# A gated recurrence and a maxout MoE, rebuilt around 128 tokens of eight heads

## The chip, the core and the metric

The kernel runs on one core of a Trainium2 chip. The metric is the device time of one launch in microseconds. Five engines take instructions from queues of their own and meet through semaphores: PE multiplies matrices (its weight loads are a row of their own, PEld, in the profile), DVE is the vector engine, ACT the scalar engine, POOL the GpSimd, and SP issues transfers. Matrix products land in PSUM, everything else lies in SBUF; both have 128 partitions.

## The reference

The first half is a gated linear recurrence for 4 batches and 8 heads over 768 tokens with 48 columns a head. Its output, eight heads side by side, is the 3072 x 384 input of a maxout layer.

```python
for t in range(S):                                 # attention; state is 48 x 48 a head
    state = alpha[:, :, t, :, None] * state + np.einsum('bhd,bhe->bhde', k[:, :, t], v[:, :, t])
    y[:, :, t] = np.einsum('bhd,bhde->bhe', q[:, :, t], state)

x = np.ascontiguousarray(attn_out.transpose(0, 2, 1, 3)).reshape(B * S, H * D)
h1 = x @ w1                                        # w1, w2: 384 x 1024
h2 = x @ w2
g = np.maximum(h1, h2)
return (g @ w_out).astype(np.float32)              # w_out: 1024 x 384
```

Inputs, weights and output are 32-bit floats.

## The kernel before

The recurrence is cut into chunks of 128 tokens. Inside a chunk it is a masked product of scaled queries and keys, between chunks a 48 x 48 state is carried. `gla_head` does all of this for one head of one batch: four loads of 768 x 48, six chunks in two groups of three, then one or two transfers that put the head's result into its partitions of `xT`, the transposed input of the MoE. It is called 32 times, and everything in it is 48 wide.

For a head: the logarithm of alpha (L86) and its sums to the chunk's end (L91, then the exponential `Rt` of L93) give the scaled keys `KL` (POOL, L102). For a group: three products with `mrec` give the logarithms' running sums in each chunk, already transposed (`csA`, L114), measured from the chunk's middle so that both signs of the exponential stay small; ACT takes both (`AAm`, L122 and L123) and the chunk's decay (`ALE`, L126). For a chunk: two transposes of q and k into 48 partitions (`qkT`, L131 and L132), a scaling (`QKs`, L134), the scores `pp` (L136), the mask (`PTm`, L138), the scaled queries for the state (`QA2`, L140), two products into `yt` (L141, L142), the state's increment (L143) and the new state (L145). The scheduler of the tile framework sets the order on each engine from the dependencies; buffers from pools (most with two or three turns) bound how far heads overlap.

When all heads are done, the PSUM pool is released and the MoE follows in six windows of 512 tokens: for each of eight slices of 128 columns three products with w1 and three with w2 (L194, L196), a copy of the first half by ACT (L198), the maximum on DVE (L199); then 32 products with w_out (L204), a copy (L209) and the store (L210). The weights are loaded first of all, on SP's queue, and cast by POOL (L65 to L67).

Logarithm and exponential are in different tables of ACT, and each change of function loads one (the ACT_TABLE_LOAD rows).

Of the kernel before, what the change touches and what calls it, by code (L numbers as in the profile page):

```python
# [8 lines left out]
FP16 = mybir.dt.float16  # L10
FP32 = mybir.dt.float32

@with_exitstack
def kernel(
# [10 lines left out]
):  # L26
    nc = tc.nc
# [3 lines left out]
    G = 3  # L31
    NG = NCH // G
    NT, DM = out.shape
    DFF = moe_w1.shape[1]

    constp = ctx.enter_context(tc.tile_pool(name="constp", bufs=1))
    wtp = ctx.enter_context(tc.tile_pool(name="wtp", bufs=1))
    xtp = ctx.enter_context(tc.tile_pool(name="xtp", bufs=1))

    ident16 = constp.tile([128, 128], FP16)  # L40
    make_identity(nc, ident16)
    u16 = constp.tile([128, 128], FP16)
    make_upper_triangular(nc, u16, val=1.0, diag=True)
    l16 = constp.tile([128, 128], FP16)
    make_lower_triangular(nc, l16, val=1.0, diag=False)
    CW = 132
    mrec = constp.tile([128, CW], FP16)
    ones64 = constp.tile([128, 128], FP16)
    nc.gpsimd.memset(ones64, 0.0)
    nc.gpsimd.memset(ones64[0:64, :], 1.0)  # L50
    nc.gpsimd.memset(mrec, 0.0)
    nc.vector.tensor_sub(out=mrec[:, 0:128], in0=u16, in1=ones64)
    nc.gpsimd.memset(mrec[:, 128:129], 1.0)
    nc.gpsimd.memset(mrec[0:64, 129:130], 1.0)

    w1f = wtp.tile([128, 3, DFF], FP32)
    w2f = wtp.tile([128, 3, DFF], FP32)
    wof = wtp.tile([128, 8, DM], FP32)
    nc.sync.dma_start(out=w1f, in_=moe_w1.rearrange("(s p) f -> p s f", p=128))
    nc.sync.dma_start(out=w2f, in_=moe_w2.rearrange("(s p) f -> p s f", p=128))  # L60
    nc.sync.dma_start(out=wof, in_=moe_w_out.rearrange("(s p) d -> p s d", p=128))
    w116 = wtp.tile([128, 3, DFF], FP16)
    w216 = wtp.tile([128, 3, DFF], FP16)
    wo16 = wtp.tile([128, 8, DM], FP16)
    nc.gpsimd.tensor_copy(out=w116, in_=w1f)  # L65
    nc.gpsimd.tensor_copy(out=w216, in_=w2f)
    nc.gpsimd.tensor_copy(out=wo16, in_=wof)  # L67

    xT = xtp.tile([128, 3, NT], FP16)

    glap = ctx.enter_context(tc.tile_pool(name="glap", bufs=3))
    glas = ctx.enter_context(tc.tile_pool(name="glas", bufs=4))
    glps = tc.alloc_tile_pool(name="glps", bufs=2, space=bass.MemoryType.PSUM)

    def gla_head(b, h):
        qf = glap.tile([128, NCH, D], FP32, tag="qf")
        kf = glap.tile([128, NCH, D], FP32, tag="kf")
        vf = glap.tile([128, NCH, D], FP32, tag="vf")
# [24 lines left out]

        S16 = glas.tile([D, D], FP16, tag="S16")
        nc.vector.memset(S16, 0.0)

        YTsb = glap.tile([D, NG, G * C], FP16, tag="YTsb")

        for g in range(NG):
            csA = glps.tile([D, G * CW], FP32, tag="csA")  # L110
            yt = glps.tile([D, G * C], FP32, tag="yt")
            for jj in range(G):
                c = g * G + jj
                nc.tensor.matmul(  # L114
                    csA[:, jj * CW : (jj + 1) * CW],
                    lhsT=loga[:, c, :],
                    rhs=mrec,
                    start=True,
                    stop=True,
                )  # L120
# [7 lines left out]
            for jj in range(G):  # L128
# [112 lines left out]
```

## Time and profile before

| | |
|---|---|
| median of 3 runs | 414.44 us (414.21 to 414.57) |
| span of the profiled execution | 412.1 us |
| PE busy, matmuls | 343.6 us, 1856 |
| DVE busy, instructions | 250.9 us, 977 |
| ACT busy, instructions | 202.9 us, 390 |
| POOL busy, instructions | 45.9 us, 82 |
| bytes moved by DMA | 31.05 MB in 107,855 packets, 101,424 of them under 512 bytes |
| granted clock of PE | 1.000 |

The span runs from the first to the last instruction. Matmuls are pipelined and their ends modelled, so a matmul's record is longer than what it keeps PE from doing; what one costs in a row of its kind is the distance from start to start. The share of busy time is a mean over a recurrence stage and a MoE stage with different limits.

### The profile page before, as it was taken

The numbers are of one execution on the slowest core, as the hardware profiler recorded it, in microseconds if no ns is written. First come the engines' busy times: TensorE is split into PE (matmuls) and PEld (weight loads), VectorE is DVE, ScalarE is ACT, GpSimd is POOL, SyncE is SP. The second block draws the span as 40 slices with busy tenths as digits, with TensorE's granted clock in tenths as the row PEclk, the third lists the DMA queues.
The fourth block names the chain that finished last, engine by engine and source line by source line (L and its number), as shares of the span: only waits on it lengthen the run. The fifth ranks groups of instructions, "written<-read, shape, count | busy, mean of one in ns | idle before, by whom it ended". The sixth has DMA issues, their size and how long they took to land. (4 is left out here: it accounts for less than half of the span.)

```text
span 412.1 us, 5933 instructions
## 1 busy us (share of the span) xinstructions
PE 343.6 (83%) x1856; PEld 181.5 (44%) x1856; DVE 250.9 (61%) x977; ACT 202.9 (49%) x390; POOL 45.9 (11%) x82
## 2 busy tenths in 40 slices
PE   0036888888888888888888888888898999999996
PEld 0013444444444444444444444444443545545543
DVE  0134777777777777777777777777884342442441
ACT  0148656556556556656556656656201344344342
POOL 4330111112111111111111111111100000000000
PEclk9999999999999999999999999999999999999999
DMA  7992253333443333443333444211000012012012
GB/s 291 280 173 43 59 105 69 67 64 67 90 97 75 64 66 65 85 99 77 66 64 64 86 96 81 51 36 37 10 13 9 21 58 76 19 59 76 21 59 76
DMA packets 107855, 31.05 MB, mean 75 GB/s; under 512 B 101424, under 2 KB 107056, under 8 KB 107824
## 3 DMA queue, kind: packets, MB, share of 16 engines
q1 hardware_dynamic: 54192, 16.52, 18.1%
q10 hardware_dynamic: 53632, 14.16, 15.5%
q8 instruction: 14, 0.23, 0.2%
q14 instruction: 17, 0.14, 0.1%
HBM read 23.59 MB, written 4.72 MB: 69 GB/s over the span
## 5 line engine op out<-in xcount | busy, mean ns | idle before, releaser
L131 PE MATMUL qkT<-ident,q 128*48 128x128 f16 x192 | 57.7, 301 | 23.7 <-DVE q L99 23.7
L138 DVE TENSOR_TENSOR PTm<-pp,u 128x128 f16<-128x128 f32 x192 | 54.8, 286 | 31.2 <-PE pp L136 22.6
L199 DVE TENSOR_TENSOR gT<-h1s,h2p 128x512 f16<-128x512 f16 x48 | 33.0, 688 | 58.1 <-ACT h1s L198 30.2
L122 ACT ACT_TABLE_LOAD x30 | 38.5, 1283 | 48.8 <-DVE QKs L134 47.6
L122 ACT ACTIVATE AAm<-csA 48x396 f16<-48x396 f32 x64 | 31.6, 494 | 59.5 <-DVE QKs L134 58.8
L132 PE MATMUL qkT<-ident,k 128*48 128x128 f16 x192 | 60.3, 314 | 0.0
L143 PE MATMUL aux<-vh,KL 128*48 128x48 f16 x192 | 45.6, 238 | 16.0 <-POOL KL L102 12.4
L141 PE MATMUL yt<-PTm,vh 128*48 128x128 f16 x192 | 52.4, 273 | 7.1 <-DVE PTm L138 5.6
L134 DVE TENSOR_TENSOR QKs<-qkT,AAm 48x256 f16<-48x256 f16 x192 | 52.9, 276 | 6.4 <-ACT AAm L123 1.9
L136 PE MATMUL pp<-QKs 48*128 48x128 f16 x192 | 54.7, 285 | 0.0
L86 ACT ACT_TABLE_LOAD x31 | 39.8, 1283 | 19.1 <-POOL vh L101 18.6
L198 ACT CAST h1s<-h1p 128x512 f16<-128x512 f32 x48 | 28.1, 586 | 42.1 <-PE h1p L194 42.1
L114 PE MATMUL csA<-mrec,loga 128*48 128x132 f16 x192 | 34.2, 305 | 17.2 <-ACT ALE L126 13.8
L142 PE MATMUL yt<-QA,S16n 48*48 48x128 f16 x160 | 47.8, 299 | 0.0
L143 PEld LDWEIGHTS <-KL 128*48 128x48 f16 x192 | 28.2, 147 | 42.4 <-POOL KL L102 24.1
L140 DVE TENSOR_SCALAR QA<-QKs,ALE 48x128 f16<-48x128 f16 x192 | 46.2, 241 | 0.0
L145 DVE SCALAR_TENSOR_TENSOR S16n<-S16n,ALE,aux 48x48 f16<-48x48 f16 x160 | 39.7, 248 | 7.3 <-PE aux L143 7.1
L131 PEld LDWEIGHTS <-q 128*48 128x48 f16 x192 | 21.7, 113 | 45.9 <-DVE q L99 23.7
L194 PE MATMUL h1p<-xT,w 128*128 128x512 f16 x144 | 40.2, 389 | 0.6 <-DVE YTsb L154 0.6
L154 DVE CAST YTsb<-yt 48x384 f16<-48x384 f32 x64 | 35.2, 550 | 8.4 <-PE yt L142 1.6
L196 PE MATMUL h2p<-xT,w 128*128 128x512 f16 x144 | 39.7, 385 | 0.0
L101 POOL CAST vh<-vf 128x288 f16<-128x288 f32 x32 | 13.6, 424 | 234.3 <-issue 228.0
(43 smaller groups left out, 370.4 us busy)
## 6 DMA issues: line engine op xcount, KB each, us to landing
kf<-in_k_dram ACTq DMA_DIRECT2D x32, 144.0 KB, 3.3
vf<-in_v_dram ACTq DMA_DIRECT2D x32, 144.0 KB, 3.3
qf<-in_q_dram SPq DMA_DIRECT2D x32, 144.0 KB, 2.6
af<-in_alpha_dram SPq DMA_DIRECT2D x32, 144.0 KB, 3.1
out_dram<-outs ACTq DMA_DIRECT2D x24, 192.0 KB, 1.9
xT<-YTsb SPq DMA_DIRECT2D x24, 72.0 KB, 3.1
w1f<-in_moe_w_dram SPq DMA_DIRECT2D x1, 1536.0 KB, 6.8
w2f<-in_moe_w_dram SPq DMA_DIRECT2D x1, 1536.0 KB, 10.7
```

The costliest lines, as they stand in the source:

```text
L86: nc.scalar.activation(out=loga, in_=af, func=mybir.ActivationFunctionType.Ln)
L122: nc.scalar.activation(out=AAm[:, 0, :], in_=csA, func=mybir.ActivationFunctionType.Exp, scale=1.0)
L131: nc.tensor.transpose(qkT[:, 0, :], q16[:, c, :], ident16)
L132: nc.tensor.transpose(qkT[:, 1, :], k16[:, c, :], ident16)
L134: nc.vector.tensor_mul(out=QKs, in0=qkT, in1=AAm[:, :, jj * CW : jj * CW + C])
L136: nc.tensor.matmul(pp, lhsT=QKs[:, 1, :], rhs=QKs[:, 0, :], start=True, stop=True)
L138: nc.vector.tensor_mul(out=PTm, in0=pp, in1=u16)
L140: nc.vector.tensor_scalar(out=QA2, in0=QKs[:, 0, :], scalar1=ALE[:, jj, 1:2], scalar2=None, op0=mybir.AluOpType.mult)
L141: nc.tensor.matmul(yt[:, jj * C : (jj + 1) * C], lhsT=vh[:, c, :], rhs=PTm, start=True, stop=False)
L142: nc.tensor.matmul(yt[:, jj * C : (jj + 1) * C], lhsT=S16, rhs=QA2, start=False, stop=True)
L143: nc.tensor.matmul(pst, lhsT=KL[:, c, :], rhs=vh[:, c, :], start=True, stop=True)
L194: nc.tensor.matmul(h1p, lhsT=w116[:, ds, fsl], rhs=xT[:, ds, tkn], start=(ds == 0), stop=(ds == 2))
```

## The change

A unit of work is now 128 tokens of one batch with all eight heads: 24 units (`gla(i)`), each with four loads that bring tokens into partitions and heads into columns. Operands are padded: each head of the logarithm, q and k has 64 columns, 48 in use, in tiles that are zeroed once, so that two heads fill 128 columns and are transposed by one instruction.

The running sum `cs` is one product for eight heads, not transposed; q and k are scaled before the transpose (`qn` on DVE, `kn` on POOL). Four products with two columns (`dps`) give the decay of each half of the chunk. After eight transposes DVE copies all of `tp` at once to `qk`. Each pair of heads then has the first head in partitions 0 to 47 and the second in 64 to 111, and the eight score products alternate between them. The state is carried for pairs: increment `kv`, `tm` on DVE, the next chunk's scaled state `sb` on POOL.

The result is built transposed, directly as MoE input. Values (`vp`) and states (`sb`) stand in wide zeroed tiles, and `vwin` and `swin` take windows of 128 columns from them in which a head's 48 columns fall where they belong in `x`. Products of several heads so accumulate into the same `yp`, sixteen a unit, ten where no state comes in. The transfers to `xT` are gone; ACT copies `yp` to `xt`.

The maxout uses max(a, b) = b + relu(a - b): the kernel forms w12 = w1 - w2 (L143) and w2o = w2 w_out (L137) once, so that a window takes one product with w12, a relu (ACT and DVE in turn), the product with w_out, and x w2o on top. A window is 256 tokens, and `moe(w)` is called after unit 2w + 3, between the units. ACT names one table at the start that holds logarithm and exponential.

All loads are on SP's queue: units 0 and 1, the weights (w2, w_out, w1), then the other units, with buffers for eight.

```diff
-    for b in range(B):
-        for h in range(H):
-            gla_head(b, h)
-    glps.release()
+    nc.scalar.preload_act_table_set("natural_log_exp_and_others")
+    def load(i):
+        b, c = divmod(i, NCH)
+        t = {}
+        for name, src in (("af", alpha), ("kf", k), ("qf", q), ("vf", v)):
+            t[name] = ldp.tile([128, H, D], FP32, tag=name, name=name)
+            nc.sync.dma_start(out=t[name], in_=src[b, :, c * C : (c + 1) * C, :].rearrange("h p d -> p h d"))
+        loads[i] = t
...
+    def vwin(t, h, ds):
+        p = 128 + h * VS - (D * h - 128 * ds)
+        return t[:, p : p + 128]
...
+    def gla(i):
...
+        nc.scalar.activation(out=lg[:, :, 0:D], in_=t["af"], func=ACTF.Ln)
+        nc.gpsimd.tensor_copy(out=vd, in_=t["vf"])
...
+        nc.tensor.matmul(csv, lhsT=mrec, rhs=lg[:, :, 0:D], start=True, stop=True)
+        for j in range(HP):
+            nc.tensor.matmul(
+                dps[:, j, :], lhsT=lg[:, 2 * j : 2 * j + 2, :].rearrange("p h w -> p (h w)"), rhs=halves,
+                start=True, stop=True,
+            )
...
+        nc.scalar.activation(out=Em, in_=csv, func=ACTF.Exp, scale=-1.0)
+        nc.scalar.activation(out=Ep, in_=csv, func=ACTF.Exp)
...
+        nc.scalar.activation(out=de, in_=dps, func=ACTF.Exp)
+        nc.gpsimd.tensor_mul(out=kn[:, :, 0:D], in0=t["kf"], in1=Em)
+        nc.vector.tensor_mul(out=qn[:, :, 0:D], in0=t["qf"], in1=Ep)
+        tp = psp.tile([128, 2, HP, C], FP16, tag="g", bufs=3, name="tp")
...
+        qk = gp.tile([128, 2, HP, C], FP16, tag="qk", name="qk")
+        nc.vector.tensor_copy(out=qk, in_=tp)
...
+                nc.gpsimd.tensor_mul(
+                    out=sd[r, :, e], in0=tm[r], in1=dd[r, :].unsqueeze(2).to_broadcast([64, HP, D])
+                )
...
+        for j in range(HP):
+            for a in range(2):
+                r = slice(64 * a, 64 * a + D)
+                nc.tensor.matmul(pa[a][:, j, :], lhsT=qk[r, 1, j, :], rhs=qk[r, 0, j, :], start=True, stop=True)
+        for a in range(2):
+            nc.vector.tensor_mul(
+                out=pt[:, a], in0=pa[a], in1=u16.unsqueeze(1).to_broadcast([128, HP, C])
+            )
...
+            mms += [(vwin(vp, h, ds), pt[:, h % 2, h // 2, :]) for h in range(H) if ds in touches(D * h, D)]
...
+    def moe(w):
...
+                    nc.tensor.matmul(
+                        hp[:, n, :], lhsT=w12[:, ds, f * 128 : (f + 1) * 128],
+                        rhs=xt[:, ds].rearrange("p n t -> p (n t)"), start=(ds == 0), stop=(ds == ND - 1),
+                    )
+            if f2 % 2 == 0:
+                nc.scalar.activation(out=gT[:, 2 * f2 : 2 * f2 + 2, :], in_=hp, func=ACTF.Relu)
+            else:
+                nc.vector.tensor_relu(out=gT[:, 2 * f2 : 2 * f2 + 2, :], in_=hp)
...
+                nc.tensor.matmul(op, lhsT=xt[:, ds, n, :], rhs=w2o[:, ds, :], start=(ds == 0), stop=False)
...
+    for i in range(NI):
+        if i + 2 < NI:
+            load(i + 2)
+        gla(i)
+        if i == 1:
+            weights()
+        if i % 2 == 1 and i // 2 - LAG >= 0:
+            moe(i // 2 - LAG)
```

The scheduler puts the instructions of two units and one MoE window into one another. On PE before, in mid-recurrence, one step of a head reads:

```order
L131 LDWEIGHTS q_987
L131 MATMUL qkT<-ident_64,q_987 48x128
L132 LDWEIGHTS k_988
L132 MATMUL qkT<-ident_64,k_988 48x128
L143 LDWEIGHTS KL
L143 MATMUL aux<-vh,KL 48x48
L141 LDWEIGHTS vh
L141 MATMUL yt<-PTm,vh 48x128
L142 LDWEIGHTS S16n
L142 MATMUL yt<-QA_1092,S16n 48x128
L136 LDWEIGHTS QKs
L136 MATMUL pp<-QKs 128x128
```

Afterwards, in unit 4 (counted from 0) with MoE window 1, PE has these rows between the last transpose of q (L177 stands ahead of two more hp) and the scores `pp` (L219), where `op` is the MoE's output:

```order
L258 LDWEIGHTS xt
L258 MATMUL op<-w2o,xt 128x384
L258 LDWEIGHTS xt
L258 MATMUL op<-w2o,xt 128x384
L258 LDWEIGHTS xt
L258 MATMUL op<-w2o,xt 128x384
L260 LDWEIGHTS gT
L260 MATMUL op<-wo_147,gT 128x384
L260 LDWEIGHTS gT
L260 MATMUL op<-wo_147,gT 128x384
L219 LDWEIGHTS qk
L219 MATMUL pp<-qk 128x128
```

The scores of a unit now stand behind five products of the MoE, which wait for nothing of that unit. In the same place the four transposes of kn stand behind ten hp products, and those of qn behind twelve more and the four kv.

On ACT before, at a change of head, with a table load at each change of function:

```order
L86 ACT_TABLE_LOAD
L86 ACTIVATE loga<-af 128x288
L82 DMA vf<-in_v_dram 128x6x48
L81 DMA kf<-in_k_dram 128x6x48
L122 ACT_TABLE_LOAD
L122 ACTIVATE AAm<-csA 48x396
L123 ACTIVATE AAm<-csA 48x396
L126 ACTIVATE ALE<-csA 48x6
L122 ACTIVATE AAm<-csA 48x396
L123 ACTIVATE AAm<-csA 48x396
```

Afterwards, from unit 3's exponentials to unit 4's:

```order
L167 ACTIVATE Em<-cs 128x384
L168 ACTIVATE Ep<-cs 128x384
L170 ACTIVATE de<-cs 128x8
L236 CAST xt<-yp 128x3x128
L153 ACTIVATE lg_123<-af 128x8x48
L263 COPY outs<-op 128x384
L236 CAST xt<-yp 128x3x128
L263 COPY outs<-op 128x384
L167 ACTIVATE Em<-cs 128x384
L264 DMA out_dram<-outs 128x2x384
L168 ACTIVATE Ep<-cs 128x384
L170 ACTIVATE de<-cs 128x8
```

Em and Ep of unit 3 come ahead of the copy of unit 2's result (the first `xt`), but those of unit 4 stand behind the copy of unit 3's, and the store of a MoE window stands between Em and Ep.

## Rows read from the trace of the kernel before

**Rows 1.** The page, part 1: busy time, share and instructions of each engine
```profile
PE 343.6 (83%) x1856; PEld 181.5 (44%) x1856; DVE 250.9 (61%) x977; ACT 202.9 (49%) x390; POOL 45.9 (11%) x82
```

**Rows 2.** Windows: busy us (x instructions) by engine, granted clock, DMA share, GB/s
```profile
3.00:10.00 7.00, 0.00 (x0) 0.00 (x0) 0.00 (x0) 0.00 (x0) 2.34 (x1) 1.00 1.02 393
24.00:30.00 6.00, 2.35 (x18) 1.42 (x17) 1.53 (x6) 4.39 (x11) 0.73 (x1) 1.00 1.43 187
100.00:200.00 100.00, 87.53 (x486) 47.42 (x487) 75.99 (x327) 58.41 (x115) 12.59 (x23) 1.00 0.37 74
330.00:411.00 81.00, 78.57 (x405) 39.41 (x403) 27.52 (x40) 33.52 (x61) 0.00 (x0) 1.00 0.15 55
```

**Rows 3.** Timeline of PE, one step in mid-run: start us, us, line, tiles, shapes
```profile
150.51 0.30 PE L131 MATMUL qkT<-ident,q 128*48 128x128 f16 x1
150.61 0.31 PE L132 MATMUL qkT<-ident,k 128*48 128x128 f16 x1
150.72 0.25 PE L143 MATMUL aux<-vh,KL 128*48 128x48 f16 x1
150.97 0.26 PE L141 MATMUL yt<-PTm,vh 128*48 128x128 f16 x1
151.16 0.30 PE L142 MATMUL yt<-QA,S16n 48*48 48x128 f16 x1
151.39 0.29 PE L136 MATMUL pp<-QKs 48*128 48x128 f16 x1
151.61 0.30 PE L131 MATMUL qkT<-ident,q 128*48 128x128 f16 x1
...
152.51 0.27 PE L114 MATMUL csA<-mrec,loga 128*48 128x132 f16 x1 [0.49 <-ACT ALE L126]
152.57 0.25 PE L143 MATMUL aux<-vh,KL 128*48 128x48 f16 x1
```

**Rows 4.** Groups of instructions, table loads of ACT: busy us, mean ns, idle before
```profile
L86 ACT ACT_TABLE_LOAD x31 | 39.8, 1283 | 19.1 <-POOL vh L101 18.6
...
L122 ACT ACT_TABLE_LOAD x30 | 38.5, 1283 | 48.8 <-DVE QKs L134 47.6 <-issue 1.2
```

**Rows 5.** Waits: who waited for whom, total us, times, longest
```profile
ACT AAm L122 <- DVE QKs L134: 58.8, 30, 3.5
```

**Rows 6.** Chain of waits, its last piece: start us, us, what
```profile
403.37 5.21 PE outp L204 x32
```

**Rows 7.** Groups by form on DVE, ACT, POOL: busy us, mean ns, idle before
```profile
L138 DVE TENSOR_TENSOR PTm<-pp,u 128x128 f16<-128x128 f32 x192 | 54.8, 286 | 31.2 <-PE pp L136 22.6
...
L134 DVE TENSOR_TENSOR QKs<-qkT,AAm 48x256 f16<-48x256 f16 x192 | 52.9, 276 | 6.4 <-ACT AAm L123 1.9
...
L199 DVE TENSOR_TENSOR gT<-h1s,h2p 128x512 f16<-128x512 f16 x48 | 33.0, 688 | 58.1 <-ACT h1s L198 30.2 <-PE h2p L196 27.9
...
L122 ACT ACTIVATE AAm<-csA 48x396 f16<-48x396 f32 x64 | 31.6, 494 | 59.5 <-DVE QKs L134 58.8 <-PE csA L114 0.4
...
L209 ACT COPY outs<-outp 128x384 f32<-128x384 f32 x24 | 11.5, 480 | 22.9 <-PE outp L204 22.9
...
L102 POOL TENSOR_TENSOR KL<-kf,Rt 128x288 f16<-128x288 f32 x32 | 23.4, 730 | 19.3 <-ACT ALE L126 7.3 <-issue 7.3 <-ACT Rt L93 4.7
...
L101 POOL CAST vh<-vf 128x288 f16<-128x288 f32 x32 | 13.6, 424 | 234.3 <-issue 228.0 <-DMA vf<-in_v_dram 6.4
```

**Rows 8.** Timeline of the start: a cast of DVE beside a cast of POOL
```profile
20.76 2.75 POOL L67 CAST wo<-wof 128x3072 f16<-128x3072 f32 x1
...
22.37 1.30 DVE L99 CAST q<-qf 128x288 f16<-128x288 f32 x1 [6.66 <-DMA qf<-in_q_dram]
...
23.72 0.12 PEld L131 LDWEIGHTS <-q 128*48 128x48 f16 x1 [23.72 <-DVE q L99]
...
25.19 0.31 DVE L99 CAST q<-qf 128x288 f16<-128x288 f32 x1 [1.51 <-DMA qf<-in_q_dram]
```

**Rows 9.** Timeline of the end: the last issue of an output
```profile
409.11 0.34 ACTq L210 DMA_DIRECT2D out_dram<-outs  x1
```

More of the change, by code (lines that the diff above doesn't have):

```diff
@@ new lines @@
+    ldp = ctx.enter_context(tc.tile_pool(name="ldp", bufs=8))
+    gp = ctx.enter_context(tc.tile_pool(name="gp", bufs=3))
+    mp = ctx.enter_context(tc.tile_pool(name="mp", bufs=2))
+    psp = ctx.enter_context(tc.tile_pool(name="psp", bufs=1, space=bass.MemoryType.PSUM))
+    nc.scalar.preload_act_table_set("natural_log_exp_and_others")
+    loads = {}
+    def load(i):
[5 more added lines that the diff above has]
+        loads[i] = t
@@ L42 @@
+    load(0)
+    load(1)
+    w2f = wp.tile([128, ND, DFF], FP32)
+    wof = wp.tile([128, NF, DM], FP32)
+    w1f = wp.tile([128, ND, DFF], FP32)
+    nc.sync.dma_start(out=w2f, in_=moe_w2.rearrange("(s p) f -> p s f", p=128))
+    nc.sync.dma_start(out=wof, in_=moe_w_out.rearrange("(s p) d -> p s d", p=128))
+    nc.sync.dma_start(out=w1f, in_=moe_w1.rearrange("(s p) f -> p s f", p=128))
     u16 = constp.tile([128, 128], FP16)
     make_upper_triangular(nc, u16, val=1.0, diag=True)
-    l16 = constp.tile([128, 128], FP16)
@@ L45 @@
[L45 to L47 removed]
+    mrec = constp.tile([128, 128], FP16)
+    halves = constp.tile([128, 2], FP16)
     ones64 = constp.tile([128, 128], FP16)
[L49 to L54, printed above, removed]
@@ new lines @@
+    nc.vector.memset(ones64, 0.0)
+    nc.vector.memset(ones64[0:64, :], 1.0)
+    nc.vector.tensor_sub(out=mrec, in0=u16, in1=ones64)
+    nc.vector.memset(halves, 0.0)
+    nc.vector.memset(halves[64:128, 0:1], 1.0)
+    nc.vector.memset(halves[0:64, 1:2], 1.0)
+    ident = constp.tile([128, 128], FP16)
+    make_identity(nc, ident)
+    NB = 3
+    LG, QN, KN, VP = [], [], [], []
+    for n in range(NB):
+        for lst, nm in ((LG, "lg"), (QN, "qn"), (KN, "kn")):
+            t = constp.tile([128, H, P64], FP16, name=f"{nm}{n}")
+            nc.gpsimd.memset(t, 0.0)
+            lst.append(t)
+        t = constp.tile([128, 128 + H * VS], FP16, name=f"vp{n}")
+        nc.gpsimd.memset(t, 0.0)
+        VP.append(t)
@@ new lines, with swin, touches @@
+    SB = []
+    for n in range(3):
+        t = constp.tile([128, 128 + HP * SS], FP16, name=f"sb{n}")
+        nc.vector.memset(t, 0.0)
+        SB.append(t)
+    def vwin(t, h, ds):
+        p = 128 + h * VS - (D * h - 128 * ds)
+        return t[:, p : p + 128]
+    def swin(t, j, ds):
+        p = 128 + j * SS - (2 * D * j - 128 * ds)
+        return t[:, p : p + 128]
+    def touches(lo, n):
+        return range(lo // 128, (lo + n - 1) // 128 + 1)
+    w2h = wp.tile([128, ND, DFF], FP16)
@@ new lines, with weights @@
+    w12 = wp.tile([128, ND, DFF], FP16)
+    wo16 = wp.tile([128, NF, DM], FP16)
+    w2T = wp.tile([128, NF, DM], FP16)
+    w2o = wp.tile([128, ND, DM], FP16)
+    def weights():
+        for ds in range(ND):
+            nc.scalar.copy(out=w2h[:, ds, :], in_=w2f[:, ds, :])
+            wt = psp.tile([128, NF, 128], FP16, tag="m", bufs=3, name="wt")
+            for f in range(NF):
+                nc.tensor.transpose(wt[:, f, :], w2h[:, ds, f * 128 : (f + 1) * 128], ident)
+            nc.vector.tensor_copy(out=w2T[:, :, ds * 128 : (ds + 1) * 128], in_=wt)
+        nc.gpsimd.tensor_copy(out=wo16, in_=wof)
+        for ds in range(ND):
+            wq = psp.tile([128, DM], FP32, tag="m", bufs=3, name="wq")
@@ L214 @@
+    LAG = 1
+    NWIN = NI // 2
+    for i in range(NI):
[6 more added lines that the diff above has]
+            moe(i // 2 - LAG)
+    for w in range(NWIN - LAG, NWIN):
+        moe(w)
 _INS = ['q', 'k', 'v', 'alpha', 'moe_w1', 'moe_w2', 'moe_w_out']
```

229 lines of the change are left out of this document (90 added, 139 removed).

## The prediction

> **What bounds the kernel now.** I read the windows first, then the waits, then the timeline of one step. The page counts PE busy 83% of the span [rows 1], but that is an average over two stages, and busy PE is not full PE. In the window from 100 to 200 us, the recurrence, PE shows 486 matmuls in 100 us [rows 2]. One step (one head, 128 tokens) issues six matmuls (L131, L132, L136, L141, L142, L143), one csA (L114), and a sixth of L91: 7.17. So 486/7.17 = 67.8 steps, 1.475 us each, and 192 steps make 283 us. The step in the timeline, from one L131 to the next, takes 1.10 us when it isn't held up [rows 3]; the rest are stops at the borders of groups and heads. Operands there are 48 columns or 48 partitions wide, so each instruction costs nearly what a full one would, and eight heads pay it eight times. ACT is no cover: it loads a table 61 times at 1.283 us [rows 4], and its exponentials wait for DVE, 58.8 us in total [rows 5]. DVE is busy 76 of 100 us there [rows 2].
>
> From 330 us on is the MoE stage. PE is dense: 32 products of 384 columns take 5.21 us [rows 6], 0.163 us each or 0.424 ns a column. A block of 512 tokens is 48 products of 512 columns (0.217 by the same rate) and these 32: 15.6 us, six blocks 94 us. The clock is granted at 1.00, the 2.4 GHz level, in every window [rows 2], so both stages ran at full clock. 283 + 94, about 27 us of start and 3 of end give 407, against a span of 412.1.
>
> **The change: work on PE.** A unit is now 128 tokens of eight heads; 24 units replace 192 steps. Prices per instruction come from pitches, start to start, in the timeline [rows 3]. Between full-height matmuls of 128 columns: 150.51 to 150.61 is 0.10, the next 0.11; the shortest, csA to L143, is 0.06. No row has 128-wide weights with 128 moving columns, so 0.06 and 0.11 are my bounds and I take 0.085, the middle. Before and behind a matmul on 48 partitions the pitch is longer: 0.19 (L141 to L142), 0.23 (L142 to L136), 0.22 (L136 to L131). The eight score products (pp) of a unit have 48 partitions each, but alternate between partitions 0 and 64. Bounds: 0.06 if the halves overlap wholly, 0.23 if they don't; I take half of 0.23, 0.116, plus 0.2 for the two changes of height.
>
> Per unit: cs 0.16; four dps with 2 columns at 0.06, 0.24; eight transposes 0.68; four kv (96 columns, 0.08) 0.32; pp 8 x 0.116 + 0.2 = 1.13; sixteen yp 1.36. Sum 3.89 us, where eight steps now take 11.8. MoE per unit: twelve hp of 256 columns at 0.108 and eleven op of 384 at 0.163: 3.09, where the rate before gives 15.6/4 = 3.9. Two units with one MoE window, the period in which the order repeats, are 2 x 6.98 = 13.96 us of PE.
>
> The Trainium skill, TensorEngine Tiling (Array Packing), Key Properties, says that a change of tiling mode drains the engine, and that separate tiles load and multiply in parallel. The trace agrees with the first half: 0.19 and 0.22 at a change against 0.10. No row here shows the second; taken at its best it gives pp the lower bound, and the sum would be 11 x 2 x 8 x 0.056 = 10 us lower.
>
> **The others have room.** A 384-column ACT operation from PSUM takes 0.48 (L209), so Ln, two exponentials, the copy of yp, the small exponential (bounded above by 0.48) and half a MoE window (two relus of 512 at about 0.6, two copies) are 5 x 0.48 + 1.08 = 3.5 us a unit. The 61 table loads become one. DVE: qn 0.5 (a 288-column cast is 0.31 in rows 8), pt 2 x 0.69 (L199), one relu 0.69, the qk copy of 1024 two-byte columns from PSUM, tm 2 x 0.35 (64 columns more than L138). The copy is open: L134 moves 256 such columns in 276 ns where L138 needs 286 for 128 of four bytes, which suggests half price, 0.68; at L138's rate it is 1.22. I take 0.95. Sum 4.2. POOL: casting v 0.57 and kn 0.97 (L101 and L102 times 384/288), two sb at 0.49, dd 0.1: 2.6 [rows 7, 8]. All are under 6.98.
>
> Loads: four tensors of 4.72 MB in the same 192-byte pieces, all on SP's queue. From 24 to 30 us the trace moves such pieces at 187 GB/s with DMA saturated [rows 2]: 18.9 MB are 101 us, 4.2 a unit, plus 0.5 of output. Hidden under 7, with buffers for eight units ahead.
>
> **Waits that remain.** PE takes its instructions in the order written, so a chain through ACT, POOL and DVE is covered only by what stands between. Handover from one engine to the next is 0.05: the cast of rows 8 ends at 23.67, PE's load starts at 23.72. A PE result is there about 0.3 after its start (the records' length in rows 3).
> - cs to the transposes of kn: 0.33 + 0.05 + Em 0.48 + 0.05 + kn 0.97 + 0.05 = 1.93. Between them the order has cs, dps and ten hp (1.48 us) in the even unit; cs, dps, six op and a yp (1.46) in the odd. Left: 0.45 twice, 0.9.
> - last transpose to pp: 0.3 + 0.05 + copy 0.95 + 0.05 = 1.35, behind two hp and five op (1.03), or five op (0.81): 0.3 + 0.55 = 0.85.
> - pp to yp: 0.3 + 0.05 + 0.69 + 0.05 = 1.1, covered in the even unit, 0.25 over in the odd.
> - qn stands on DVE beside kn on POOL. A cast of SBUF on DVE took 1.30 us beside a POOL cast, 0.31 alone, and ended 0.16 after POOL [rows 8]. So qn ends after kn, about 2.4 after cs; the four transposes of kn (0.34) come first. 0.2 per period.
>
> Together 2.2, so the period is 16.2 us. The Trainium skill, GPSIMD Engine Reference, Specifications, has the last as a rule: POOL's SBUF interfaces are shared with VectorE, contended by its instructions with two SBUF inputs. Without it the sum would be 2 us lower; if the whole 0.5 of each qn were exposed, 11 x 2 x 0.5 - 2 = 9 higher.
>
> **Sum.** Start: data flow from 3 us [rows 2]; two units 8.4, then weights 4.72 MB at 393 GB/s 12.0, so w1 lands at 23.4; then w1 - w2, three times 1.2 on DVE (L199 carried on to 1024 columns): 27, with unit 2's cs done. Zeroing the padded tiles on POOL, three sets of 3,072 columns at the 2.75 of L67 [rows 8], takes 8.3 us and ends before. Units 0 and 1 and the weight products fit in those 27; as a period starts with cs and hp I count it from 26. Then eleven periods, units 2 to 23 with MoE windows 0 to 10: 178. Then window 11 alone: 24 x 0.108 + 22 x 0.163 = 6.2, 0.8 for its relu, and copy, issue and transfer: 412.1 - 409.11 + 0.5 + 0.5 = 4 [rows 9]. Span 26 + 178 + 11 = 215. The median of the runs, 414.44, lies 2.3 above the profiled span of 412.1; so **217 us**.
>
> **Rivals.**
> - *PE denser than I price it.* All 128-column pitches and pp at 0.06: per unit cs 0.16, dps 0.24, transposes 0.48, kv 0.24, pp 0.68, yp 0.96, so 2.76 + 3.09; twice 11.7, waits 2.2: 13.9 a period, 153 + 37 + 2.3 = 192. For it: the 0.06 pair and the wholly hidden weight loads at 384 columns. Against: shorter fill uncovers more of the same chains.
> - *The chains decide.* pp at 0.23 (+1.8 a period), the copy at 1.22 (+0.5), kn a third slower, as both its inputs are now four bytes (+0.65): 19.2 a period, 211 + 37 + 2.3 = 250. For it: pitches of 0.19 to 0.23 are all that rows 3 show on 48 partitions.
> - *Slower than before, by POOL.* Its tiles are now rows of eight pieces of 48 columns, where L101 and L102 had one stretch. If each piece costs an instruction's price rather than its columns', a unit (24 pieces) at 0.73 each is 17.5 us, a period 35, and 11 x 35 + 37 + 2.3 = 424. It decides from 0.71 a piece. Against: L102's 2.5 ns a column already looks like a loop over columns; no row shows POOL on pieces.
>
> **How the numbers follow.** Forecast 0.60, denser 0.20, chains 0.18, POOL 0.02. The last alone is slower. The forecast's own bounds are about 203 to 232; the range reaches into both next cases, 186 to 250. Under 0.2%, 0.8 us, a measurement can't be told from no change. Faster 0.97, within 0.2% 0.01, slower 0.02.
>
> **What would show it.** A period (Em of one even unit to the next) near 16 us; PE dense but for stops of 0.3 to 0.6 us before the transposes and before pp; POOL's kn near 0.97 and qn ending after it; yp pitches of 0.085; the first hp near 27 us; one table load; granted clock 1.00. Wrong would be a period under 14 or over 19, loads landing late after 30 us, or PE waiting longer for yp's copy or a relu than for kn.

## The result, and the profile after

The changed kernel takes **187.5 us** (median of four runs, 187.3 to 189.69) where the kernel before takes 414.5 beside it (414.21 to 414.73): ratio 0.454, interval 0.4516 to 0.4564. I had forecast 217, with 186 to 250 around it, and 192 if PE were denser than I priced it. Where the runs of a kernel fall into faster and slower ones, a time given below is that of the faster ones. The profiled execution of the changed kernel has a span of 185.5 us; the 11 periods that I counted lie between 31.2 and about 175 us.

The groups of instructions by form, in which [rows 7] are answered (columns: line, engine, operation, output and inputs, count; then busy us, mean ns, idle time before and what ended it):

```profile
L171 POOL TENSOR_TENSOR kn<-kf,Em 128x384 f16<-128x384 f32 x24 | 23.9, 995 | 79.2 <-ACT Em L167 59.4 <-issue 19.8
L172 DVE TENSOR_TENSOR qn<-qf,Ep 128x384 f16<-128x384 f32 x24 | 21.1, 878 | 14.1 <-ACT Ep L168 10.6 <-ACT de L170 3.1 <-issue 0.3
...
L181 DVE COPY qk<-tp 128x1024 f16<-128x1024 f16 x24 | 16.5, 689 | 14.3 <-PE tp L177 12.9 <-PE kv L200 1.0
...
L58 ACT ACT_TABLE_LOAD x1 | 1.3, 1283 | 0.7 <-PEq L294 0.7
```

The 61 table loads of [rows 4] are one. kn on POOL has the price that I carried over by columns (995 ns, forecast 970), so POOL doesn't pay per piece. qn on DVE has not the price I gave it: 878 ns on average where I took 500. The qk copy takes 689 ns, the cheap end of my 0.68 to 1.22.

By windows, against [rows 2] (busy us and instructions of PE, PE's loads, DVE, ACT, POOL; granted clock; DMA share; GB/s):

```profile
22.00:25.00 3.00, 0.72 (x9) 0.32 (x9) 1.27 (x3) 0.00 (x0) 2.85 (x4) 0.94 1.33 215
25.00:28.00 3.00, 2.91 (x12) 1.53 (x13) 2.90 (x5) 0.14 (x1) 0.03 (x1) 0.50 1.45 189
90.00:120.00 30.00, 25.57 (x291) 17.89 (x288) 18.62 (x32) 12.09 (x32) 13.09 (x22) 1.00 1.11 184
120.00:150.00 30.00, 26.55 (x288) 18.56 (x287) 16.66 (x29) 13.04 (x32) 10.47 (x18) 1.00 0.55 97
```

From 90 to 150 us PE is busy 25.6 to 26.6 of 30 us, at full clock. DMA is saturated to 120 us, as forecast, and hides: from 31 us on no wait in the trace is for a load. The stretch from 22 to 28 us is new: PE is busy 0.72 of 3 us, and then the granted clock is 0.50, the 1.2 GHz level.

PE in the odd unit 13, start to start, against the step of [rows 3] (start us, us, line, tiles, shapes):

```profile
102.95 0.32 PE L159 MATMUL cs<-lg,mrec 128*128 128x384 f16 x1
103.11 0.24 PE L161 MATMUL cs<-halves,lg 128*128 128x2 f16 x4
103.22 0.48 PE L260 MATMUL op<-wo,gT 128*128 128x384 f16 x2
103.54 0.66 PE L232 MATMUL yp<-pt,vp 128*128 128x128 f16 x9
104.04 0.33 PE L260 MATMUL op<-wo,gT 128*128 128x384 f16 x1
105.01 0.40 PE L177 MATMUL tp<-ident,kn 128*128 128x128 f16 x4 [0.65 <-POOL kn L171]
105.24 0.29 PE L200 MATMUL kv<-vp,kn 128*128 128x96 f16 x3
...
106.61 0.40 PE L219 MATMUL pp<-qk 48*128 48x128 f16 x8
106.97 0.28 PE L232 MATMUL yp<-qk,sb 128*128 128x128 f16 x2
```

Nine yp take 103.54 to 104.04: 0.056 each. The four transposes of kn take 0.23, four kv in a row 0.17 (below, 85.74 to 85.91), four dps 0.11, and eight pp 0.36 from their first start to yp's (0.33 in most units); the products of 384 columns keep their 0.16. One full stop remains in this unit, before the transposes of kn: cs starts at 102.95 and the transposes at 105.01, a chain of 2.06 us (forecast 1.93).

In unit 13 the copy of qk ends just before pp, so what the change of height costs is read in unit 3, where the copy had ended 0.58 before (DVE's copy, and PE up to 41.07):

```profile
39.79 0.69 DVE L181 COPY qk<-tp 128x1024 f16<-128x1024 f16 x1 [0.60 <-PE tp L177]
...
40.80 0.33 PE L260 MATMUL op<-wo,gT 128*128 128x384 f16 x1
41.06 0.23 PE L219 MATMUL pp<-qk 48*128 48x128 f16 x2
```

pp starts 0.26 behind the product of 384 columns, not 0.16: about 0.1 for the change. By 41.07 two pp have started: the records of single products have them 0.003 us apart, one in each half of the partitions, and such pairs 0.056 to 0.066 apart. The two halves work side by side, and a pair costs what one full-height product does. Behind the last pp comes another 0.1: yp starts 0.15 after it, not 0.056.

All engines in the even unit 12:

```profile
84.45 1.00 POOL L171 TENSOR_TENSOR kn<-kf,Em 128x384 f16<-128x384 f32 x1 [0.45 <-ACT Em L167]
...
84.79 1.07 DVE L172 TENSOR_TENSOR qn<-qf,Ep 128x384 f16<-128x384 f32 x1 [2.42 <-ACT Ep L168]
...
85.51 0.40 PE L177 MATMUL tp<-ident,kn 128*128 128x128 f16 x4 [0.55 <-POOL kn L171]
...
85.74 0.33 PE L200 MATMUL kv<-vp,kn 128*128 128x96 f16 x4
...
85.91 0.27 PE L246 MATMUL hp<-xt,w 128*128 128x256 f16 x1
...
86.00 1.08 POOL L194 TENSOR_TENSOR sb<-tm,dd 64x192 f16<-64x192 f32 x2
86.02 0.39 PE L177 MATMUL tp<-ident,qn 128*128 128x128 f16 x4
...
86.54 0.35 DVE L209 TENSOR_TENSOR tm<-kv,sb 64x192 f32<-64x192 f32 x1 [0.67 <-POOL sb L194]
87.12 0.36 DVE L209 TENSOR_TENSOR tm<-kv,sb 64x192 f32<-64x192 f32 x1 [0.23 <-POOL sb L194]
...
87.51 0.69 DVE L181 COPY qk<-tp 128x1024 f16<-128x1024 f16 x1
...
88.26 0.40 PE L219 MATMUL pp<-qk 48*128 48x128 f16 x8 [0.76 <-DVE qk L181]
```

qn (DVE) begins beside kn (POOL), takes 1.07 and ends 0.4 after it. Its transposes come at 86.02; then the qk copy doesn't run at once, because in DVE's queue the two tm stand before it, and they wait for the two sb on POOL. The copy starts at 87.51, and pp, on which PE waits, at 88.26. Who waits for whom, in total:

```profile
PEld L177 <- POOL kn L171: 26.0, 22, 6.3
...
PEld L219 <- DVE qk L181: 10.3, 22, 1.3
...
PE hp L246 <- ACT xt L236: 1.1, 2, 0.5
```

(26.0 includes the start, with one stop of 6.3.) Waits for kn are PE's largest by far; relus and yp's copy cost it 1.1. The last issue of an output is at 182.17, 3.3 us before the end of the span, where it was 3.0 [rows 9].

The start of the changed kernel, where the forecast of 26 us for the first period failed:

```profile
20.64 3.07 POOL L133 CAST wo<-wof 128x3072 f16<-128x3072 f32 x1
...
23.95 1.08 POOL L194 TENSOR_TENSOR sb<-tm,dd 64x192 f16<-64x192 f32 x2
...
25.09 0.39 PE L232 MATMUL yp<-qk,sb 128*128 128x128 f16 x2 [1.00 <-POOL sb L194]
...
25.28 2.12 PE L137 MATMUL wq<-wo,w2T 128*128 128x384 f16 x6
...
29.06 2.28 PE L137 MATMUL wq<-wo,w2T 128*128 128x384 f16 x13
...
31.18 0.33 PE L159 MATMUL cs<-lg,mrec 128*128 128x384 f16 x1
```

The cast of wo, 3.07 us on POOL, stands there in front of unit 1's dd and sb; yp of unit 1 waits for sb, and the first weight products (L137) behind it run at half clock: six took 2.12 us, where the last thirteen, at full clock again, took 2.28 (0.16 each). cs of unit 2 starts at 31.18.

### The profile page after: what moved, and what is told of

It reads as the page before. It is cut to its first block, busy times and chain, and to the rows that moved or that the text cites. A ratio compares the mean times of both kernels' runs of the same rounds, so it can differ in the third digit from the quotient of the medians.

```text
span 185.5 us, 3954 instructions
## 1 busy us (share of the span) xinstructions
PE 145.4 (78%) x1544; PEld 101.6 (55%) x1544; DVE 102.6 (55%) x175; ACT 73.8 (40%) x175; POOL 75.9 (41%) x129
## 5 line engine op out<-in xcount | busy, mean ns | idle before, releaser
L171 POOL TENSOR_TENSOR kn<-kf,Em 128x384 f16<-128x384 f32 x24 | 23.9, 995 | 79.2 <-ACT Em L167 59.4
L260 PE MATMUL op<-wo,gT 128*128 128x384 f16 x192 | 40.6, 326 | 0.0
L246 PE MATMUL hp<-xt,w 128*128 128x256 f16 x288 | 38.9, 272 | 1.7 <-ACT xt L236 1.1
L221 DVE TENSOR_TENSOR pt<-pp,u 128x512 f16<-128x512 f32 x48 | 30.9, 685 | 6.2 <-PE pp L219 5.7
L246 PEld LDWEIGHTS <-w 128*128 128x128 f16 x288 | 26.1, 97 | 5.9 <-issue 3.2
L172 DVE TENSOR_TENSOR qn<-qf,Ep 128x384 f16<-128x384 f32 x24 | 21.1, 878 | 14.1 <-ACT Ep L168 10.6
L232 PE MATMUL yp<-pt,vp 128*128 128x128 f16 x240 | 26.3, 223 | 1.1 <-DVE pt L221 0.8
L177 PE MATMUL tp<-ident,kn 128*128 128x128 f16 x96 | 10.7, 229 | 19.5 <-POOL kn L171 19.5
L260 PEld LDWEIGHTS <-gT 128*128 128x128 f16 x192 | 16.9, 97 | 9.9 <-issue 1.8
L194 POOL TENSOR_TENSOR sb<-tm,dd 64x192 f16<-64x192 f32 x40 | 20.3, 506 | 2.9
L177 PEld LDWEIGHTS <-kn 128*128 128x128 f16 x96 | 6.1, 100 | 26.0 <-POOL kn L171 26.0
L232 PEld LDWEIGHTS <-vp 128*128 128x128 f16 x240 | 18.2, 100 | 3.3 <-issue 0.2
L167 ACT ACTIVATE Em<-cs 128x384 f32<-128x384 f32 x24 | 11.8, 493 | 18.8 <-PE cs L161 18.8
## 6 DMA issues: line engine op xcount, KB each, us to landing
wof<-in_moe_w_out_dram SPq DMA_DIRECT2D x1, 1536.0 KB, 10.5
```

Source lines behind the costliest of these rows:

```text
L171: nc.gpsimd.tensor_mul(out=kn[:, :, 0:D], in0=t["kf"], in1=Em)
L172: nc.vector.tensor_mul(out=qn[:, :, 0:D], in0=t["qf"], in1=Ep)
L177: nc.tensor.transpose(tp[:, n, j, :], src[:, 2 * j : 2 * j + 2, :].rearrange("p h w -> p (h w)"), ident)
L194: nc.gpsimd.tensor_mul(out=sd[r, :, e], in0=tm[r], in1=dd[r, :].unsqueeze(2).to_broadcast([64, HP, D]))
L221: nc.vector.tensor_mul(out=pt[:, a], in0=pa[a], in1=u16.unsqueeze(1).to_broadcast([128, HP, C]))
L232: nc.tensor.matmul(yp[:, ds, :], lhsT=l, rhs=r, start=(n == 0), stop=(n == len(mms) - 1))
```

## The experiments

The ratios are against the kernel before in runs of the same set; the changed kernel's is 0.454. "Period" is from one Em of an even unit to the next, as in the prediction, from unit 2 to unit 22, divided by ten. In the changed kernel it is (162.68 - 31.75)/10 = 13.09 us. The scheduler orders PE's instructions anew for each edit, so a difference is that of the edit together with its order. Of the theories on record before each run, A came for kn (a little beyond its range), the start, both together, the algebra and the table load, and B for the split copy and the single heads; for the order of the halves B's time came. The three runs on the interleaving went otherwise, as said there.

**The chain through kn.** kn moved from POOL to DVE:
```
-        nc.gpsimd.tensor_mul(out=kn[:, :, 0:D], in0=t["kf"], in1=Em)
+        nc.vector.tensor_mul(out=kn[:, :, 0:D], in0=t["kf"], in1=Em)
```

> kn is computed by DVE instead of POOL. Theory A (the chain through kn, 1.0 us on POOL, and qn held beside it to 1.1 us, makes PE's remaining waits): kn and qn take about 0.55 each one after the other, PE's wait for kn falls from 26 us in total to under 12, the period from 13.1 to about 12.3, time 175 to 181 us. Rival B (DVE's queue decides: 0.55 more per unit in front of the copy of tp and the masks): the waits move to the copy and the time is 186 to 193.

Measured: 174.16 us, ratio 0.4202 (0.4178 to 0.4226). The groups by form, and then the waits:

```profile
L172 DVE TENSOR_TENSOR qn<-qf,Ep 128x384 f16<-128x384 f32 x24 | 13.5, 564 | 1.7 <-ACT Ep L168 1.7
L171 DVE TENSOR_TENSOR kn<-kf,Em 128x384 f16<-128x384 f32 x24 | 13.5, 563 | 25.2 <-ACT Em L167 25.1
```

```profile
PEld L177 <- DVE kn L171: 8.8, 14, 1.7
```

kn takes 563 ns instead of 995, and qn behind it 564 instead of 878: without kn on POOL beside it qn takes 0.64 of the time on average. PE's loads wait 8.8 us for kn, not 26.0, and the period is (149.48 - 30.75)/10 = 11.87, 1.2 shorter. Their wait for the copy of qk stays, 10.2 us against 10.3, and is now the largest. So the chain through kn did set the larger part of the stops, and the engine that I had judged by its room (POOL, 2.6 of 7 us) was the one that made the chain long.

**The start.** The cast of wo moved off POOL:
```
-        nc.gpsimd.tensor_copy(out=wo16, in_=wof)
+        for n in range(4):
+            nc.scalar.copy(out=wo16[:, 2 * n : 2 * n + 2, :], in_=wof[:, 2 * n : 2 * n + 2, :])
```

> The cast of w_out at the start is done by ACT (four pieces) instead of POOL. In the changed kernel POOL casts from 20.6 to 23.7 us, then makes the first scaled state; unit 2's cs starts at 31.2 us, where 25 to 27 was predicted. Theory A (that cast holds back state, result and weight products): unit 2's cs by 29 us, time 2 to 4 us less, 183.5 to 185.5. Rival B (the landing of the weights and PE's weight products set the start): cs near 31, time 187.5 within 1.

Measured: 185.16 us (185.12 to 185.28), ratio 0.4472 (0.4464 to 0.448). In the window that had 0.50:

```profile
25.00:28.00 3.00, 3.00 (x33) 2.16 (x31) 3.00 (x4) 1.92 (x5) 0.00 (x0) 1.00 1.41 190
```

The clock stays at 1.00 and cs of unit 2 starts at 27.56, 3.6 us earlier. Of these about 2.1 arrive at the end of the span (183.4 against 185.5), since the periods that follow are 0.15 longer. How much of the 3.6 is the clock's can be estimated from the run with all windows behind the units (the second run under "The interleaving"): it has the same cast and the same stretch with PE busy 0.72 of 3 us, yet keeps full clock:

```profile
22.00:25.00 3.00, 0.72 (x9) 0.32 (x9) 1.20 (x3) 0.00 (x0) 2.85 (x4) 1.00 1.30 218
25.00:28.00 3.00, 2.77 (x28) 2.04 (x29) 2.76 (x5) 0.92 (x3) 0.18 (x1) 1.00 1.43 191
```

There cs of unit 2 starts at 29.89, so about 1.3 of the 3.6 go with the clock and the rest with the cast itself. Why the clock fell in one of the two and not in the other these runs don't show.

**Both together.** 

> kn on DVE (e2) and the cast of w_out on ACT (e8) together. Theory A (two separate waits, one per unit, one at the start): 174.2 - 2.3 = 171 to 173 us. Rival B (with kn off POOL the cast at the start already comes sooner, so the second adds nothing): 173.5 to 175.

Measured: **171.55 us** (171.04 to 173.03), ratio 0.4142 (0.4126 to 0.4157): the gains add up within the spread of the runs (13.3 + 2.3 of 187.5 leaves 171.8). It is the fastest version here.

**Splitting the qk copy** on top of both:
```
-        nc.vector.tensor_copy(out=qk, in_=tp)
+        nc.scalar.copy(out=qk[:, 1], in_=tp[:, 1])
+        nc.vector.tensor_copy(out=qk[:, 0], in_=tp[:, 0])
```

> As the run before, and the copy of the transposes is split: ACT copies the half of kn, DVE that of qn. Theory A (the copy of 0.69 us is on the chain to pp, and the halves run beside each other): 0.2 to 0.4 less per unit, 164 to 169 us. Rival B (ACT takes the half late, behind other copies in its queue, and PE is near its own 10.6 a period): 170 to 175 us.

Measured: 174.4 us, ratio 0.4211 (0.4199 to 0.4224), 3 us slower than without it. Sharing this link with a second engine did not pay here. That ACT comes late with its half, as theory B has it, fits but is not shown: I didn't follow ACT's queue.

**What PE's small products cost.** The eight pp in order of halves, four on partitions 0 to 47 first:
```
-        for j in range(HP):
-            for a in range(2):
+        for a in range(2):
+            for j in range(HP):
```

> The eight score products of a unit run as four on partitions 0 to 47 and then four on 64 to 111, instead of alternating; nothing else changes. In the changed kernel the burst of eight alternating ones takes 0.40 us (0.05 each), not the 1.13 that was predicted. Theory A (the two halves of the array overlap, so alternating is what makes them cheap): within one half each costs 0.10 to 0.23 as on 48 partitions before, the burst 0.8 to 1.8 us, the time 195 to 215 us. Rival B (the price follows from the weights' width and the columns, whichever half): burst 0.40 to 0.45, time 187.5 within 1.

Measured: 187.34 us, ratio 0.4533 (0.4513 to 0.4553), no difference. PE's timeline:

```profile
107.13 0.41 PE L219 MATMUL pp<-qk 48*128 48x128 f16 x8
107.48 0.28 PE L232 MATMUL yp<-qk,sb 128*128 128x128 f16 x2
```

From pp to yp is 0.35, as with alternating halves (0.33 to 0.36). The low price of pp does not come from the order of halves, but from their overlap, which the order does not change. In the records the eight start in pairs here too, 0.013 apart, and pairs again about 0.056 apart. Of the eight as written, the fourth and the eighth signal DVE; in the records those two start seventh and eighth. So the second half does not wait until the first is through: between the halves PE did not keep to the written order. Theory A had the overlap right and wrongly tied it to alternating.

One transpose per head in place of one per pair, with halves alternating (first) and apart (second):
```
-                nc.tensor.transpose(
-                    tp[:, n, j, :], src[:, 2 * j : 2 * j + 2, :].rearrange("p h w -> p (h w)"), ident)
+                for a in range(2):
+                    nc.tensor.transpose(tp[64 * a : 64 * a + 64, n, j, :], src[:, 2 * j + a, :], ident)
```

> q and k are transposed one head at a time, sixteen transposes a unit with 64-column weights instead of eight with 128; the rest is the same. Eight paired ones now take 0.46 us (0.057 each), where before the change 48-column weights showed 0.09 to 0.11. Theory A (narrow weights load slowly, and that made the small matmuls dear): sixteen at about 0.10 are 1.6 us, PE 1.1 us more a unit, time 203 to 215 us. Rival B (the price is that of 128 moving columns, 0.057, whatever the weights): 0.46 us more a unit, part of it in waits, 190 to 199 us.

> Sixteen single-head transposes as in e6, but the four first heads of the pairs, then the four second ones, so that neighbours write the same half of the array's columns. In e6, where neighbours alternated between the halves, eight took 0.41 us as recorded, 0.027 each, no more than four paired ones, so neither theory of e6 was tested on a pitch. Theory A (64-column weights load behind the product before them when both are in one half, as the 48-column ones before the change at 0.09 to 0.11): sixteen take 1.5 us, time 198 to 212 us. Rival B (no such cost): pitch at or under 0.057, sixteen under 0.95 us, time 189 to 196.

Measured: 191.78 us, ratio 0.4623 (0.4605 to 0.4642), and 192.53, ratio 0.4647 (0.4635 to 0.4659). PE's timeline of the second:

```profile
100.83 0.42 PE L178 MATMUL tp<-ident,kn 128*64 128x128 f16 x8 [0.68 <-POOL kn L171]
101.18 0.34 PE L199 MATMUL kv<-vp,kn 128*128 128x96 f16 x4
```

Eight transposes of one head take 0.35 (100.83 to 101.18) where four of a pair take 0.23. In the records they start in pairs as pp do, 0.003 apart in the first run and 0.013 in the second, and the pairs 0.056 apart (0.08 for the first): two single heads beside each other cost what one pair does. The difference is mostly in the step to the next full-width product, 0.15 behind the last transpose where it is 0.056 behind a pair's: a change of width costs about 0.1, like the change of height at pp. The period is 13.48 in the first of the two, 0.39 more; the 16 extra transposes in it are 4 x 0.12 = 0.48. So pairing is worth 4 to 5 us of the 227 gained. Why products with 48-column weights stood 0.10 apart in the kernel before, where those of one half are 0.056 apart here, is not settled by these runs.

**The algebra of the maxout** taken back: products with w1 and w2, a copy on ACT, a maximum on DVE, and no w2 times w_out:
```
-            hp = psp.tile(...)            # one product with w1 - w2
-            ... relu on ACT (even) or DVE (odd)
+            for wx in (w12, w2h): ...     # two products (w12 holds w1)
+            nc.scalar.copy(out=h1s, in_=hps[0])
+            nc.vector.tensor_max(out=gT[...], in0=h1s, in1=hps[1])
...
-                nc.tensor.matmul(op, lhsT=xt[:, ds, n, :], rhs=w2o[:, ds, :], start=(ds == 0), stop=False)
```

> The maxout is computed as before the change, in the new order: products with w1 and with w2, a copy by ACT, the maximum on DVE, no w2 w_out and no x w2o. Per period PE has 24 x 0.108 more and 6 x 0.163 less, 1.6 us; the weight stage loses 24 transposes and 24 products, about 5 us of PE. Theory A (PE's own work passes on in full): 187.5 + 12 x 1.6 - 3 = 200 to 206 us. Rival B (the period is set by chains, 2.5 us of waits a period take the extra work): 184 to 190 us.

Measured: 202.66 us, ratio 0.4893 (0.4879 to 0.4907): the algebra is worth 15 us. The period is 14.58, 1.49 more. Per window 24 products of 256 columns come and six of 384 go: 24 x 0.109 - 6 x 0.163 = 1.64. That is what one would see if PE's work passes on almost in full, though PE stands still for parts of each period; but the edit also gives ACT and DVE four operations each a window where they had two, and no run separates the two.

**The table load.** The line that loads one table for both functions is removed:
```
-    nc.scalar.preload_act_table_set("natural_log_exp_and_others")
```

> The one line that names a table for ACT at the start is left out; the order built then has 41 table loads on ACT, one ahead of a logarithm and one ahead of the exponentials in most units, about 51 us at 1.283 each. Theory A (ACT stands in the chain from cs to kn, so a good part of a load shows in each unit): period up by 1.3 to 3, time 202 to 222 us. Rival B (ACT is idle for 60% of the span and loads in that time): 187 to 191 us.

Measured: 218.45 us, ratio 0.5265 (0.5223 to 0.5307). The groups by form:

```profile
L152 ACT ACT_TABLE_LOAD x21 | 26.9, 1283 | 4.2 <-DMA af<-in_alpha_dram 3.9
L166 ACT ACT_TABLE_LOAD x21 | 26.9, 1283 | 6.7 <-PE cs L160 6.4
```

41 more loads at 1.283 us are 52.6 us of ACT, and 31 us arrive in the time, though ACT had been busy 40% only: Ln and the exponentials are links of the chain through kn (PE's loads wait 47.5 us for it, not 26.0). A part goes with the clock, whose mean is 0.937 here and 0.990 in the changed kernel: from unit 16 to unit 20, at 1.00 throughout, two periods take 29.2 us against 25.5, 1.85 more each, where the mean over ten is 2.9 more.

**The interleaving.** First all MoE blocks are written last, with buffers for it:
```
-    LAG = 1
+    LAG = NI // 2
```

> All MoE windows stand behind the last unit (twelve xt buffers instead of four); the work is the same. Theory A (the windows fill PE's waits in a unit): the units alone run at the length of their chain, cs to cs about 4.3 us, so 31 + 22 x 4.3 + twelve windows at 6.2 = 200 to 206 us. Rival B (units fill each other's waits just as well, PE's total decides): 185 to 190 us.

Measured: 186.81 us, ratio 0.4513 (0.45 to 0.4525). The windows written last do not run last: the scheduler pulls them forward into the units, as PE's timeline shows (hp among yp), so the run doesn't decide what the interleaving is worth.

```profile
70.10 0.22 PE L232 MATMUL yp<-pt,vp 128*128 128x128 f16 x1
70.15 0.38 PE L246 MATMUL hp<-xt,w 128*128 128x256 f16 x2
```

Then the MoE gets its PSUM in a pool that opens only after the units' pool is released:
```
+    psp.release()
+    psm = ctx.enter_context(tc.tile_pool(name="psm", bufs=1, space=bass.MemoryType.PSUM))
```

> The run with the windows written last (e3) came out at 186.8 us, since the scheduler moved them forward among the units: that run did not take the interleaving away. Here the MoE has its own PSUM pool, opened when the units' pool is released, as before the change, so that no window can start ahead of the last unit. Theory A (windows fill waits): units run at their chain, about 4.3 to 4.8 us, then twelve dense windows at 6.2: 31 + 22 x 4.5 + 74 + 4 = 203 to 213 us. Rival B (interleaving has no part in the gain): 184 to 191 us.

Measured: 242.35 us (the others 246.26 to 247.33), against 413.81 for the kernel before: 55 more than with interleaving, and beyond both theories. By windows:

```profile
60.00:100.00 40.00, 29.33 (x273) 22.63 (x274) 25.88 (x41) 12.44 (x35) 19.95 (x34) 0.50 1.29 185
...
160.00:200.00 40.00, 38.95 (x286) 27.72 (x284) 8.99 (x13) 13.44 (x25) 0.00 (x0) 1.00 0.16 60
```

With the units alone the granted clock falls to 0.50, the 1.2 GHz level, and comes back at 1.00 in the MoE. A unit takes (143.65 - 64.18)/14 = 5.68 us, where 4.3 to 4.8 was expected. So two units and one window are 2 x 5.68 + 6.2 = 17.6 us in turn and 13.09 interleaved; 12 times the difference is 54 of the 55.

Is it the clock or the chains? The same kernel with ten products of 512 columns more per unit, whose result is never read:
```
+            for n in range(5):
+                nc.tensor.matmul(fl, lhsT=ident, rhs=w2h[:, n % ND, 0:512], start=True, stop=True)
```

> As e9 (all windows behind all units), with ten products of 512 columns a unit from unit 2 on whose results nobody reads, 2.2 us of PE at 2.4 GHz. e9 had units 5.65 us apart at a granted clock of 0.50 from 60 to 140 us, with 78 us of windows behind them, 246 us in all. Theory A (with nothing to fill PE the clock falls to 1.2 GHz, and that is a good part of what interleaving is worth): the clock stays at 1.00, units come 4.3 to 5.0 us apart, 216 to 232 us, faster than e9 with more work. Rival B (the chain through the other engines sets the units, the clock hardly counts): units 5.5 or more, 243 to 260 us.

Measured: 231.81 us, ratio 0.5598 (0.5577 to 0.5619). By windows:

```profile
60.00:100.00 40.00, 35.17 (x380) 21.24 (x381) 26.96 (x45) 14.09 (x39) 22.30 (x37) 1.00 1.19 179
```

The clock is back at 1.00 and the kernel is 10.5 us faster than the same without them (242.35) with 2.2 us more work per unit on PE, but a unit still takes (142.66 - 63.38)/15 = 5.29 us, 0.39 less. The time lies in A's range, the unit's length in neither's. The unread products (fl) are themselves in the way, as DVE's copy and PE show:

```profile
102.67 0.69 DVE L185 COPY qk<-tp 128x1024 f16<-128x1024 f16 x1 [1.02 <-PE tp L181]
...
103.81 0.40 PE L227 MATMUL pp<-qk 48*128 48x128 f16 x8
```

The copy ends at 103.36 and pp starts 0.45 later, behind fl and kv; in 16 of 22 units it is that much or more. So the 0.39 is a lower bound for the clock's part of the 2.2 us that a unit loses without interleaving ((2 x 5.68 + 6.2 - 13.09)/2). If the whole 0.45 came off, a unit at full clock would take about 4.8, which gives the clock 0.8 and the chains through ACT, POOL and DVE 1.4; this is an estimate, and no run has the units alone at full clock. The interleaved MoE is worth both: what it puts into the stops, and the clock that it keeps up.

**What has no run.** The parts taken back one at a time are worth 55 us (interleaving), 31 (table load), 15 (algebra) and 4 to 5 (pairing), and need not add. What units of eight heads bring by themselves, the largest part of the 227, was not taken back: that it is the price of PE's products is read from the two timelines.

## Why the prediction was right or wrong

**Right in kind.** Eight heads in one unit take less than half of eight steps of 1.475 us (11.8; a period less its MoE window leaves 13.09/2 - 3.09 = 3.5 a unit), PE remains the busiest engine, every other engine has room, the loads are saturated and hidden, one table load is left, the MoE window is 3.09 us per unit as priced, and the tail, from the first hp of window 11 at 174.98, is 10.5 us (forecast 11). Of the signs that I had named as wrong one came: the period is under 14 us.

**Wrong: the price of PE's products.** The step that failed is "0.06 and 0.11 are my bounds and I take 0.085, the middle", and with it pp at 1.13. Forecast and measured per unit: dps 0.24 and 0.11, transposes 0.68 and 0.45, kv 0.32 and 0.17, pp 1.13 and 0.44, yp 1.36 and 0.90. They are 1.66 us a unit, 37 us over eleven periods. The rate of the dense stage, 0.424 ns a column [rows 6], gives 0.054 for 128 columns and 0.041 for 96; measured are 0.056 and 0.043. I had that rate, used it for the MoE, and did not use it for the short products, because the recurrence had pitches of 0.10 and 0.11 [rows 3]. Those came from a stage with 48 columns of weights and stops; its one pitch of 0.06, behind 132 columns, was the rate too. A middle between them had nothing for it. That each narrow instruction "costs nearly what a full one would" was too kind to it: 0.10 to 0.23 there against 0.056 here. The number of products fell only from 57 (8 x 7.17) to 41 for 128 tokens of eight heads, their price, stops included, from 11.8/57 = 0.21 us to 3.5/41 = 0.08. The denser rival, 192 us, took 0.06 and 0.68 for pp, and is nearest to what happened; that the result lies within 186 to 250 it owes to the room left for this rival.

On pp, the Trainium skill, TensorEngine Tiling (Array Packing), Key Properties, said both that a change of mode drains and that separate tiles load and multiply in parallel. The trace agrees with the first (about 0.1 at the entry of pp, 0.26 against 0.16 in unit 3, and 0.1 behind it) and with the second: one pp of each half starts within 0.003 us, and a pair takes 0.056. So the overlap was whole, and my bound for that, 0.06 a product, was twice the price: it is 0.06 a pair. That the halves overlap when they are written apart is shown too, and is more than I read from the page.

**Right in sum, wrong in composition: the waits.** Forecast 2.2 us a period, left over 13.09 - 2 x (2.23 + 3.09) = 2.45. That the sums agree is luck. The chain to kn was right within 0.13, but its fill is shorter on a denser PE, so it costs more than the 0.9 (PE's idle time before the transposes of kn, from unit 2 to unit 22, is 12.8 us in the trace, 1.3 a period, without the 0.17 by which each record before a stop outlasts its pitch). The qk copy is cheaper than I took, but I did not see that in even units tm stands before it in DVE's queue and waits for sb on POOL. That qn ends after kn and costs little was right; the Trainium skill's GPSIMD Engine Reference, Specifications, has the reason, shared interfaces, and the runs agree: qn took 1.07 to 1.13 when it started beside kn, and 0.54 to 0.56 with POOL idle. The one that starts second pays, in this trace: POOL's small dd took 0.20 alone and 0.51 behind a running qn, a cast of vp 0.50 and, started beside a running qn, 0.83 to 0.91. kn, always the first, took 0.99 to 1.00 beside qn and also in eight even units where DVE was idle all through it.

**Wrong: the start,** 31.2 and not 26. I had counted the landing of the weights and the subtraction, and left out the cast of wo on POOL in front of unit 1's sb, and the half clock that followed. Together they cost 3.6 us there (the experiment on the start).

**The sum again:** 217 - 37 (PE) + 3 (waits) + 5 (start) is 188, against 187.5.

**The rivals.** "The chains decide" at 250 failed by pp (0.44) and the copy (0.69); POOL per piece failed by kn's 995 ns. That the chains matter nonetheless is what the fastest version shows: 16 us lie in one multiplication and one cast, both on POOL.

## What to carry to other kernels

Price short products by the rate per column of a dense stage (here good down to 96 columns; products of 2 columns still cost 0.025), with what a change of shape costs beside it, rather than by pitches from a stage that is full of stops; where two rows differ, ask what differs before taking a middle. An engine that is busy 40% of the time can still be the costliest link of a chain: look at which operation PE waits for, and try it on the engine that does it fastest, also when that one is busier. Work of another stage between the links of a chain fills the stops and keeps the clock up; check in the timeline that the scheduler has put it where you think.

## What was not expected of the hardware

- Full-height products with 128 columns of weights and 128 moving columns follow each other at 0.056 us, each with a weight load of its own: the rate of 384 columns (0.163) holds down to 96 (0.043). With 2 columns (dps) they are 0.025 apart.
- Products on partitions 0 to 47 and 64 to 111 run side by side, a pair in 0.056 us, whether they are written in turn or four and four. Entering and leaving them costs about 0.1 us each; so does leaving transposes with 64 columns of weights.
- With the units alone PE's granted clock is 0.50, and unread products bring it to 1.00 and make the kernel 10.5 us faster (242.35 to 231.81).
- A stretch of 3 us at the start with PE busy 0.72 was followed by half clock in the changed kernel, and by full clock in the run with all windows behind the units.
- A DVE multiplication of 384 four-byte columns takes 0.56 with POOL idle and up to 1.13 when it starts beside one of POOL, which itself takes 1.00 either way, so that on DVE both take little longer in turn (1.13) than kn alone does on POOL.
